# Attention followed by a long convolution on one core: shared-key scores and the last queries' value products in quarters of the TensorE array

## The chip, the cores and the metric

The kernel runs on one NeuronCore of a Trainium2 chip, in one launch. The metric is device time in microseconds (us). Engines go by their profile names: PE is TensorE's matmuls, PEld its loads of the stationary operand, DVE VectorE, ACT ScalarE, POOL GpSimd, SP SyncE, which issues most DMAs.

## The reference

Attention over 8 batches of 12 heads, 448 positions, head size 64, with one more term in the softmax's denominator, and on its output a gated convolution over the 448 positions by FFT:

```python
batch, n_heads, seq, head_dim = (8, 12, 448, 64)
scores = scale * np.matmul(q, k.transpose(0, 1, 3, 2))
m = np.max(scores, axis=-1, keepdims=True)
e = np.exp(scores - m)
attn = e / (np.sum(e, axis=-1, keepdims=True) + np.exp(-m) + 1e-09)
attn_out = np.matmul(attn, v)
x = attn_out.transpose(0, 2, 1, 3).reshape(B, S, H * D)          # 8 x 448 x 768
proj = x @ w_proj                                                # w_proj 768 x 2304
x1, x2, x3 = proj[..., :D], proj[..., D:2 * D], proj[..., 2 * D:]  # here D = 768
x2_conv = np.fft.irfft(np.fft.rfft(x2, n=S, axis=1) * np.fft.rfft(filter_fft, n=S, axis=0), n=S, axis=1)
return (x1 * x2_conv * x3) @ w_out                               # w_out 768 x 768
```

Inputs and output are float32; the kernel multiplies in bfloat16 and accumulates in float32.

## The kernel before

**Attention, pair by pair.** Two heads make a pair, numbered `i = 6 * b + hp` over 8 batches `b` and 6 pairs `hp`; head `u` of a pair is 0 or 1. In `kT` and `qT` the 64 features of head 0 lie on partitions 0 to 63 and those of head 1 on 64 to 127. The 448 keys of a head are three blocks of 128 (`t` = 1, 2, 3) and 64 left over. The left-over keys of both heads share block `t` = 0: its stationary operand is 128 x 128, with head 0's keys in one diagonal 64 x 64 block, head 1's in the other, and zeros elsewhere. `scores(0)` is thus one full-array matmul (L885), 128 rows by 128 columns, that streams 448 queries. `scores(t)` for the other blocks is two half-array matmuls (L883), one per head: 64 rows (features), 128 columns (keys), 448 queries; the heads lie on different row halves and write two banks of PSUM. `exps(t)` (ACT, L896 and L902) takes the exponential from PSUM into `e` (blocks 1 to 3, both heads) or `er` (block 0).

**Value products.** The exponentials are the stationary operand, 128 keys by 128 queries, and the values `vn` stream: 65 columns, 64 features and a column of ones for the denominator. `out_rests` (L914) does block 0: for four query blocks `n` and two heads one half-array matmul, 8 per pair. `out_rest(u)` (L922) does blocks 1 to 3 of head `u`: 12 full-array matmuls, 24 per pair. The fourth query block has 64 real queries; its other 64 columns are padding. The results of head 0 and 1 stand in two banks (`out_banks`). `norm` (DVE, L935 to L937) adds 1 to the denominators, takes reciprocals and multiplies into `xb`.

**The rest.** `x_dma` (SP, L989) turns three pairs of `xb` at once into `xT` by a DMA transpose; batch 0 does it on PE. `dense(b)` holds projections, spectra, inverse transforms and output projections (L1218, L1117, L1095, L1166, L1265, L1031), interleaved with the attention of later batches. After the last attention a flag on the smallest denominator is read and every engine takes a branch (L1573); the last output projections come after it.

**What sets the order.** Every step is a task, entered with `add(engine, cost, ...)`, what it needs, makes, and which buffers it takes and gives back. `Plan.run` plays the tasks on the engines with these costs, hands out the eight PSUM banks, and emits the instructions engine by engine. The table `plan.ORDER` holds each task's rank on its engine; the engines then run strictly in that order and wait on semaphores. A task's `rows` (64 or 128) tells the plan that a change between half and full array costs `SWITCH`. `fillers` puts idle matmuls (L1513) into PE gaps of the first 44 us of the plan.

Of the kernel before, what the change touches and what calls it, by code (L numbers as in the profile page):

```python
# [29 lines left out]
SX = 512  # L30
# [8 lines left out]
BLK_K = [FQ, FQ, SP, SP]  # L39


class Plan:
# [11 lines left out]
    LANDING = 1  # L54
    DELAY = (1.786, 2.77)
    EARLY = ((0.0, 0.0), (0.0, 0.0))
    TURN_ROOM = 1.6
# [8 lines left out]
    BRANCH = 0.0  # L66
    SWITCH = 0.093
# [16 lines left out]
    def add(self, eng, cost, want, emit, need=(), make=(), take=(), give=(), dma=0.0, run=256, n=1, after=0.0, begun=(), late=0.0, turn=False, part=None, keep=False, port=False, rows=128):  # L84
        want = self.ORDER[len(self.tasks)] if self.ORDER else want + self.SHIFT.get(part, 0.0)
        if eng == "SP":
            dma *= self.STRETCH
        if eng == "DVE" and port:
            cost += self.SHARED
        cost, dma, run, late = self.TIMES.get(len(self.tasks), (cost, dma, run, late))  # L90
        self.tasks.append((want, len(self.tasks), eng, cost, emit, need, make, take, give, dma, after, run, n, begun, late, turn, keep, port or eng == "POOL" and not dma, rows))

    def run(self):
# [21 lines left out]
        ahead = sum(t[2] == "ACT" and not t[16] for t in self.tasks)  # L115
        last = 0.0
# [80 lines left out]
        def ready(t):  # L197
            e = t[2]
            if not self.ORDER and t[10] > now + 1e-9:
                return False  # L200
            if t[16] and self.BRANCH:
                if ahead or "flag" not in when or max(last, when["flag"][0]) + self.BRANCH > now + 1e-9:
# [24 lines left out]
        while any(queue.values()):  # L227
            moved = False
            for e in queue:
# [30 lines left out]
                if e == "ACT" and not t[16]:  # L260
                    ahead, last = ahead - 1, now
                    heapq.heappush(events, now + self.BRANCH)
                if "flag" in t[6]:
                    heapq.heappush(events, end + self.BRANCH)
# [24 lines left out]
        full = self.fillers(order, gone)  # L289
        for i, (_, t) in enumerate(order):  # L290
            if i in full:
# [37 lines left out]
def kernel(  # L329
# [127 lines left out]
    flag = const.tile([1, 1], I32, name="flag")  # L457

    psum = psp.tile([128, 8 * 512], F32, name="psum")
# [33 lines left out]

# [1131 lines left out]
```

## Time and profile before

| | |
|---|---|
| runs | median 365.8 us, 365.61 to 366.53 |
| the profiled execution | 366.52 us, its span 364.7 us, granted TensorE clock 0.999 |
| PE, PEld | 356.0 us busy (98%), 211.6 (58%) |
| DVE, ACT, POOL | 259.6 us (71%), 263.8 (72%), 114.0 (31%) |
| DMA | 69.19 MB, mean 190 GB/s |
| shared-key scores (L885) | 48 matmuls of 128x448, 355 ns each |
| other scores (L883) | 288 of 64x448, 354 ns each |
| value products (L922, L914) | 1104 of 128x65, 194 ns, and 368 of 64x65, 191 ns, beside 64 that read the buffer in `wout_bf` |

The matmul's duration runs from its start to the end of its last result, while the next one is already under way; what it takes of PE's time is the distance between two starts. Times in a timeline count from the start of the span. A group `xN` of the timeline begins with its first instruction and ends with its last.

### The profile page before, as it was taken

To read this page: it belongs to the slowest core of one execution; us is meant where nothing else is said; L and a number is where in the kernel's file an instruction comes from. 1 tells how busy PE (TensorE), PEld (TensorE's weight loads), DVE (VectorE), ACT (ScalarE), POOL (GpSimd) and SP (SyncE) were. 2 spreads that over 40 slices of the span, in tenths; PEclk is the share of its full clock that TensorE was granted. 3 is DMA by queue.
4 is the path that set the end of the run, shared out by engine and by line. 5 is a ranking of instruction groups with operands and counts; after the bars stand their busy time and mean duration, and the time that the engine had idled before them with its cause. 6 is when DMAs were issued, how large, how long until landed. Compare 5 with 4: busy or idle time off the path is not lost. (4 is left out here: it accounts for less than half of the span.)

```text
span 364.7 us, 9337 instructions
## 1 busy us (share of the span) xinstructions
PE 356.0 (98%) x3599; PEld 211.6 (58%) x3600; DVE 259.6 (71%) x671; ACT 263.8 (72%) x453; POOL 114.0 (31%) x247
## 2 busy tenths in 40 slices
PE   8979999999999999999999999999999999999995
PEld 7656666656664555655565455655556556565552
DVE  6568489884889449797577568794578677858660
ACT  6879878677887588975779577878787875455443
POOL 6784463224724533444324533601020000000000
PEclk9999999999999999999999999999999999999999
DMA  8999999999999999999899999892983084143215
GB/s 219 262 245 234 257 229 205 227 199 172 220 265 257 228 250 247 227 279 212 225 240 244 271 235 221 231 216 66 190 155 68 2 151 111 43 88 88 86 49 174
DMA packets 135298, 69.19 MB, mean 190 GB/s; under 512 B 91917, under 2 KB 131664, under 8 KB 135248
## 3 DMA queue, kind: packets, MB, share of 16 engines
q1 hardware_dynamic: 130528, 62.90, 75.7%
q0 software_dynamic: 4480, 5.41, 8.7%
q8 instruction: 29, 0.48, 0.6%
q10 hardware_dynamic: 240, 0.23, 0.3%
q14 instruction: 21, 0.17, 0.2%
HBM read 43.86 MB, written 11.01 MB: 150 GB/s over the span
## 5 line engine op out<-in xcount | busy, mean ns | idle before, releaser
L896 ACT ACTIVATE e<-psum 128x896 bf16<-128x896 f32 x138 | 122.8, 924 | 20.6 <-PE psum L883 18.2
L1218 PE MATMUL psum<-xT,wproj_bf 128*128 128x448 bf16 x576 | 122.0, 353 | 0.0
L1218 PEld LDWEIGHTS <-wproj_bf 128*128 128x128 bf16 x576 | 54.4, 98 | 47.7 <-issue 3.5
L1031 PE MATMUL psum<-wout_bf,yT 128*128 128x384 bf16 (+2 forms) x287 | 54.2, 326 | 0.8 <-issue 0.6
L1117 PE MATMUL psum<-xf,wproj_bf 128*128 128x456 bf16 x216 | 45.4, 356 | 0.0
L922 PE MATMUL psum<-vn,e 128*128 128x65 bf16 x1104 | 45.2, 194 | 0.0
L922 PEld LDWEIGHTS <-e 128*128 128x128 bf16 x1104 | 39.5, 98 | 7.6 <-issue 3.4
L680 POOL CAST nat<-nat 112x512 bf16<-112x512 f32 x36 | 24.0, 671 | 62.1 <-DMA nat<-in_q_dram 61.9
L1344 ACT COPY osb<-psum 128x384 f32<-128x384 f32 (+2 forms) x56 | 25.8, 483 | 22.7 <-PE psum L1031 17.1
L883 PE MATMUL psum<-qT,kT 64*128 64x448 bf16 x288 | 41.6, 354 | 0.0
L1178 ACT CAST xs<-psum 113x384 bf16<-113x384 f32 (+1 forms) x64 | 29.6, 484 | 12.4 <-PE psum L1166 9.4
L1031 PEld LDWEIGHTS <-yT 128*128 128x128 bf16 x288 | 26.7, 98 | 20.1 <-issue 3.4
L1184 DVE TENSOR_TENSOR t<-xs,hrs 112x768 bf16<-112x768 bf16 (+1 forms) x64 | 35.3, 578 | 3.9 <-ACT xs L1178 3.7
L1234 DVE TENSOR_TENSOR g<-x,psum 128x448 bf16<-128x448 bf16 x42 | 25.8, 618 | 17.0 <-PE psum L1218 11.9
L937 DVE TENSOR_TENSOR xb<-psum,den 128x512 bf16<-128x512 f32 x48 | 33.2, 692 | 1.7
L1232 ACT CAST x<-psum 128x448 bf16<-128x448 f32 x42 | 22.3, 535 | 15.2 <-PE psum L1218 14.6
L712 POOL CAST vn<-nat 128x192 bf16<-128x192 f32 x58 | 23.1, 430 | 27.6 <-DMA nat<-in_v_dram 27.4
L1117 PEld LDWEIGHTS <-wproj_bf 128*128 128x128 bf16 x216 | 20.2, 98 | 18.8 <-issue 1.1
L1274 ACT CAST cr<-psum 128x452 bf16<-128x452 f32 x48 | 24.1, 544 | 8.1 <-PE psum L1265 7.2
L902 ACT ACTIVATE er<-psum 128x448 bf16<-128x448 f32 x46 | 25.4, 554 | 5.7 <-PE psum L885 5.4
L935 DVE TENSOR_SCALAR den<-psum 128x8 f32<-128x8 f32 x48 | 7.9, 164 | 24.1 <-PE psum L922 20.2
L700 POOL CAST nat<-nat 128x384 bf16<-128x384 f32 x29 | 16.6, 581 | 23.8 <-DMA nat<-in_k_dram 17.1
(138 smaller groups left out, 479.6 us busy)
## 6 DMA issues: line engine op xcount, KB each, us to landing
nat<-in_q_dram SPq DMA_DIRECT2D x47, 224.0 KB, 4.5
out_dram<-osb SPq DMA_DIRECT2D x23, 384.0 KB, 3.3
nat<-in_k_dram SPq DMA_DIRECT2D x41, 192.0 KB, 4.6
nat<-in_v_dram SPq DMA_DIRECT2D x41, 192.0 KB, 4.5
wproj_bf<-in_moe_w_proj_dram POOLq DMA_DIRECT2D x2, 1152.0 KB, 12.4
rests<-in_k_dram SPq DMA_DIRECT2D x8, 192.0 KB, 4.8
rests<-in_v_dram SPq DMA_DIRECT2D x8, 192.0 KB, 4.6
out_dram<-osb SPq DMA_DIRECT2D x8, 192.0 KB, 3.7
```

The costliest lines, as they stand in the source:

```text
L883: nc.tensor.matmul(sc[:, u, 0:S], kT[b % 2][c, hp, t, :], qT[b % 2][c, hp, :])
L896: nc.scalar.activation(to, of, AF.Exp, scale=SCALE)
L902: nc.scalar.activation(to, of, AF.Exp, scale=SCALE)
L922: nc.tensor.matmul(out_bank(u)[:, n, :], P["e"][1 + t][:, u * S + n * 128 : u * S + n * 128 + 128], vn[b % 2][:, hp, 4 * u + t, :], start= ...
L937: nc.vector.tensor_tensor(W["xb", b][:, hp].rearrange("p n (u d) -> p u n d", u=2), op[:, :, :, 0:DH], rec[:].unsqueeze(3).to_broadcast([1 ...
L1031: nc.tensor.matmul(ops[:n, : c.stop - c.start], y[:, dt, 0:n], wout_bf[:, dt, c], start=(dt == 0), stop=(dt == NDT - 1),)
L1117: nc.tensor.matmul(pps, wproj_bf[:, kt, D + dt * 128 : D + (dt + 1) * 128], W["xf", b][:, kt], start=(kt == 0), stop=(kt == NDT - 1),)
L1178: nc.scalar.copy(L["xs", par, ch][:K, pg % 2, :], L["Z", pg, ch][:K, :DCH])
L1184: nc.vector.tensor_tensor(t[:K], L["xs", par, ch][:K], h, op=ALU.mult)
L1218: nc.tensor.matmul(p[:, :S], wproj_bf[:, kt, 2 * part * D + dt * 128 : 2 * part * D + (dt + 1) * 128], xT()[:, kt, 0:S], start=(kt == 0), ...
L1234: nc.vector.tensor_tensor(g[:, dt, :], L["x1", dt], p[:, :S], op=ALU.mult)
L1344: (nc.vector.tensor_copy if half else nc.scalar.copy)(L["os", st][:n, c.start + lo : c.start + hi], L["O", st, ch][:n, lo:hi])
```

## The change

Four things change from batch 1 on (`QUADS`).

1. The shared-key scores of two neighbouring pairs are computed by one task, with four matmuls on quarters of the array (64 rows by 64 columns, 448 queries): per pair two, one per head, without the blocks of zeros. The second pair's heads are exchanged in their place among the columns, so that the four use the four quarters. Two PSUM banks are taken at once. `rest_values` exchanges the left-over values of the odd pairs accordingly, with three POOL copies for one.
2. The value products of the last 64 queries leave `out_rest`, which goes from 12 to 9 matmuls per head, and go into `out_rests`, in quarters: 64 keys by 64 queries. Head 0 goes to partitions 0 to 63, head 1 to 64 to 127; the two halves of the keys go to the two banks.
3. `norm` therefore first copies the second bank's part (65 columns) to SBUF and adds it to the first's. After `x_dma`, the new `x_shift` copies head 1's last 64 queries to their partitions.
4. A run of half-array tasks on PE that holds a quarter task is cut into quarters throughout (`narrow`, `parts`): a score matmul of 64 x 128 becomes two of 64 x 64.

The plan's costs, its model of the branch and its DMA delays get other values, and the whole table of ranks is new.

```diff
+QUADS = range(1, B)
-    LANDING = 1
-    DELAY = (1.786, 2.77)
+    LANDING = 1.84
+    DELAY = (0.897, 2.824)
-    SWITCH = 0.093
+    SWITCH = 0.105
...
         full = self.fillers(order, gone)
+        narrow, run = set(), []
+        for _, t in order:
+            if t[2] != "PE":
+                continue
+            if t[18] == 128:
+                run = []
+                continue
+            run.append(t[1])
+            if not self.quads.isdisjoint(run):
+                narrow.update(run)
...
-    plan.ORDER = (1, 0, 2, 125, 3, 4, 0, 0, 1, 2, 3, 4, 1, 9, 3, 0, ...
+    plan.ORDER = (1, 0, 1, 123, 3, 4, 0, 0, 3, 1, 2, 4, 2, 5, 16, 0, ...
-    plan.BRANCH = 3.5
+    plan.BRANCH = (2.5, 4.6, 2.0, 0.25)
...
+    def parts():
+        return [slice(0, 64), slice(64, 128)] if plan.narrow else [slice(0, 128)]
+
+    def rest_values(b):
+        if b not in QUADS:
+            nc.gpsimd.tensor_copy(vn[b % 2][:, :, 3, 0:DH], rests[:, 1])
+            return
+        lo, hi = slice(0, 64), slice(64, 128)
+        nc.gpsimd.tensor_copy(vn[b % 2][:, 0::2, 3, 0:DH], rests[:, 1, 0::2])
+        for to, of in ((lo, hi), (hi, lo)):
+            nc.gpsimd.tensor_copy(vn[b % 2][to, 1::2, 3, 0:DH], rests[of, 1, 1::2])
...
+        odd = hp % 2 if b in QUADS else 0
+        full = NST - 1 if b in QUADS else NST
         def scores(t):
             if t:
                 sc = pair(("sc", ("S", i, t)))
                 for u in range(2):
                     c = slice(64 * u, 64 * u + 64)
-                    nc.tensor.matmul(sc[:, u, 0:S], kT[b % 2][c, hp, t, :], qT[b % 2][c, hp, :])
+                    for m in parts():
+                        nc.tensor.matmul(sc[m, u, 0:S], kT[b % 2][c, hp, t, m], qT[b % 2][c, hp, :])
+            elif b in QUADS:
+                for g in range(2):
+                    for u in range(2):
+                        c, m = (slice(64 * x, 64 * x + 64) for x in (u, u ^ g))
+                        nc.tensor.matmul(
+                            bank(("hy", ("S", i + g, 0)))[m, 0:S], kT[b % 2][c, hp + g, 0, c], qT[b % 2][c, hp + g, :]
+                        )
...
         def out_rests():
-            for n in range(NST):
+            for n in range(full):
                 for u in range(2):
-                    c = slice(64 * u, 64 * u + 64)
+                    c = slice(64 * (u ^ odd), 64 * (u ^ odd) + 64)
+                    for m in parts():
+                        nc.tensor.matmul(
+                            out_bank(u)[m, n, :], P["e"][0][c, n * 128 + m.start : n * 128 + m.stop], vn[b % 2][c, hp, 3, :],
+                            start=(n == 0), stop=False,
+                        )
+            if full < NST:
+                q = slice(384, S)
+                half = [slice(0, 64), slice(64, 128)]
+                for u in range(2):
+                    c = half[u ^ odd]
                     nc.tensor.matmul(
-                        out_bank(u)[:, n, :], P["e"][0][c, n * 128 : n * 128 + 128], vn[b % 2][c, hp, 3, :],
-                        start=(n == 0), stop=False,
+                        out_bank(u)[half[u], full, :], P["e"][0][c, q], vn[b % 2][c, hp, 3, :], start=False, stop=False,
                     )
+                for t in (0, 2, 1):
+                    for r in range(2):
+                        for u in range(2):
+                            nc.tensor.matmul(
+                                out_bank(r ^ odd)[half[u], full, :],
+                                P["e"][1 + t][half[r], u * S + q.start : u * S + q.stop],
+                                vn[b % 2][half[r], hp, 4 * u + t, :],
+                                start=False, stop=False,
+                            )
 
         def out_rest(u):
-            for n in range(NST):
+            for n in range(full):
...
         def norm():
+            if full < NST:
+                nc.vector.tensor_copy(other, op[:, 1, full])
+                nc.vector.tensor_tensor(op[:, 0, full], op[:, 0, full], other, op=ALU.add)
...
+        def x_shift(gs):
+            nc.vector.tensor_copy(xT()[64:128, gs, 384:S], xT()[0:64, gs, S:SX])
```

Three places in the program's order show it. First, PE early in batch 2, where a shared-key score is issued (`kT`, `qT` keys and queries, `e` exponentials, `vn` values, `yT` the gated convolution that the output projection reads). Before, one full-array matmul stands between value products:

```order
L922 LDWEIGHTS e_100
L922 MATMUL psum<-vn_94,e_100 128x65
L885 LDWEIGHTS kT_89
L885 MATMUL psum<-qT_91,kT_89 128x448
L922 LDWEIGHTS e_99
L922 MATMUL psum<-vn_94,e_99 128x65
```

Now the run of half-array tasks there begins with a score block cut into quarters, and the quarter group follows it (each load and matmul that is shown of L925 and L930 stands four times):

```order
L989 LDWEIGHTS e_100
L989 MATMUL psum<-vn_94,e_100 128x65
L925 LDWEIGHTS kT_89
L925 MATMUL psum<-qT_91,kT_89 64x448
...
L930 LDWEIGHTS kT_89
L930 MATMUL psum<-qT_91,kT_89 64x448
...
L1115 LDWEIGHTS yT
L1115 MATMUL psum<-wout_bf,yT 128x384
```

The shared scores went from a full-array run into a half-array run, and two pairs' scores stand at one place. Second, PE at the value products of a pair of batch 1 (`er` the exponentials of block 0, `e` those of blocks 1 to 3). Before, eight L914 matmuls are followed, here after a score block, by the 24 of L922:

```order
L914 LDWEIGHTS er_103
L914 MATMUL psum<-vn_94,er_103 128x65
L883 LDWEIGHTS kT_90
L883 MATMUL psum<-qT_92,kT_90 128x448
...
L922 LDWEIGHTS e_99
L922 MATMUL psum<-vn_94,e_99 128x65
L922 LDWEIGHTS e_101
L922 MATMUL psum<-vn_94,e_101 128x65
```

Now twelve quarters of L964 (of which one is shown) are followed by two of L973 and by four for each key block of L979, and the full-array products of L989 come after:

```order
L964 LDWEIGHTS er_102
L964 MATMUL psum<-vn_94,er_102 64x65
...
L973 LDWEIGHTS er_102
L973 MATMUL psum<-vn_94,er_102 64x65
...
L979 LDWEIGHTS e_96
L979 MATMUL psum<-vn_94,e_96 64x65
...
L979 LDWEIGHTS e_98
L979 MATMUL psum<-vn_94,e_98 64x65
...
L989 LDWEIGHTS e_96
L989 MATMUL psum<-vn_94,e_96 128x65
```

Work of all four key blocks went into the quarter run, and of the full-array products nine instead of twelve per head are left. Third, DVE at a normalisation of batch 1. Before:

```order
L604 COPY qT_92<-psum 128x448
L593 COPY kT_90<-psum 128x512
L935 TENSOR_SCALAR den_108<-psum 128x8
L936 RECIPROCAL den_108<-den_108 128x8
L937 TENSOR_TENSOR xb<-psum,den_108 128x2x4x64
```

Now:

```order
L642 COPY qT_92<-psum 128x448
L1002 COPY other<-psum 128x65
L1003 TENSOR_TENSOR psum<-psum,other 128x65
L1005 TENSOR_SCALAR den_108<-psum 128x8
L1006 RECIPROCAL den_108<-den_108 128x8
L1007 TENSOR_TENSOR xb<-psum,den_108 128x2x4x64
```

Two instructions came in ahead of each normalisation.

More of the change, by code (lines that the diff above doesn't have):

```diff
@@ L65 @@
     PORT = 0.16
-    BRANCH = 0.0
-    SWITCH = 0.093
+    BRANCH = ()
+    SWITCH = 0.105
     NBANKS = 8
@@ L82, in __init__, with add @@
         self.rows = {}
-    def add(self, eng, cost, want, emit, need=(), make=(), take=(), give=(), dma=0.0, run=256, n=1, after=0.0, begun=(), late=0.0, turn=False, part=None, keep=False, port=False, rows=128):
+        self.quads = set()
+        self.narrow = False
+    def add(self, eng, cost, want, emit, need=(), make=(), take=(), give=(), dma=0.0, run=256, n=1, after=0.0, begun=(), late=0.0, turn=False, part=None, keep=False, port=False, rows=128, quad=False):
+        if quad:
+            self.quads.add(len(self.tasks))
         want = self.ORDER[len(self.tasks)] if self.ORDER else want + self.SHIFT.get(part, 0.0)
@@ L114, in run @@
         clock = 0.0
-        ahead = sum(t[2] == "ACT" and not t[16] for t in self.tasks)
-        last = 0.0
+        ahead = {e: sum(t[2] == e and not t[16] for t in self.tasks) for e in ("ACT", "PE")}
+        last = {"ACT": 0.0, "PE": 0.0}
         landed = {"SP": [], "POOL": []}
@@ L201, in ready @@
             if t[16] and self.BRANCH:
-                if ahead or "flag" not in when or max(last, when["flag"][0]) + self.BRANCH > now + 1e-9:
+                if "flag" not in when:
+                    return False
+                at = when["flag"][0] + self.BRANCH[0]
+                if e != "PE":
+                    if ahead["ACT"] or ahead["PE"]:
+                        return False
+                    at = max(when["flag"][0] + self.BRANCH[1], last["ACT"] + self.BRANCH[2], last["PE"] + self.BRANCH[3])
+                if at > now + 1e-9:
                     return False
@@ L259, in run @@
                 heapq.heappush(events, end)
-                if e == "ACT" and not t[16]:
-                    ahead, last = ahead - 1, now
-                    heapq.heappush(events, now + self.BRANCH)
+                if e in ahead and not t[16]:
+                    ahead[e] -= 1
+                    last[e] = now if e == "ACT" else end
+                    for x in self.BRANCH:
+                        heapq.heappush(events, last[e] + x)
                 if "flag" in t[6]:
-                    heapq.heappush(events, end + self.BRANCH)
+                    for x in self.BRANCH:
+                        heapq.heappush(events, end + x)
                 for k in t[13]:
@@ L457 @@
     flag = const.tile([1, 1], I32, name="flag")
+    other = const.tile([128, DH + 1], F32, name="other")
     psum = psp.tile([128, 8 * 512], F32, name="psum")
@@ L926, in out_rest @@
                         start=False,
-                        stop=(n == NST - 1 and t == 1),
+                        stop=(n == full - 1 and t == 1),
                     )
@@ L952, in rests @@
         def rests(j, w):
-            add("PE", 0.125, w, T[j]["rests"], need=[("e", j), ("ones", j // NHP % 2), "pads", ("v", j), ("vr", j // NHP)], make=[("ER", j)],
-                take=[("op", j)], give=[("er3" if j in THIRD else "er", (j, 0))], rows=64)
+            add("PE", 0.235 if j // NHP in QUADS else 0.125, w, T[j]["rests"], need=[("e", j), ("ones", j // NHP % 2), "pads", ("v", j), ("vr", j // NHP)], make=[("ER", j)],
+                take=[("op", j)], give=[("er3" if j in THIRD else "er", (j, 0))], rows=64, quad=j // NHP in QUADS)
         for t in range(4):
             w = tau(i, t / 4 if i or t else 1.0)
-            add("PE", 0.195 if t else 0.19, w, lambda t=t: scores(t),
-                need=[("kT", i), ("qT", i)] + ([("S", i - 1, 2)] if b and not t else []) + ([] if i or t else ["kT0"])
-                + ([("S", i, t - 1) if t > 1 else ("S", i - 1, 3)] if t and (i or t > 1) else []),
-                make=[("S", i, t)], take=[(ring(t), ("S", i, t))], rows=64 if t else 128)
+            if t or b not in QUADS:
+                add("PE", 0.195 if t else 0.19, w, lambda t=t: scores(t),
+                    need=[("kT", i), ("qT", i)] + ([("S", i - 1, 2)] if b and not t else []) + ([] if i or t else ["kT0"])
+                    + ([("S", i, t - 1) if t > 1 else ("S", i - 1, 3)] if t and (i or t > 1) else []),
+                    make=[("S", i, t)], take=[(ring(t), ("S", i, t))], rows=64 if t else 128)
+            elif not odd:
+                add("PE", 0.22, w, lambda t=t: scores(t),
+                    need=[(x, j) for j in (i, i + 1) for x in ("kT", "qT")] + [("S", i - 1, 2)],
+                    make=[("S", j, 0) for j in (i, i + 1)], take=[("hy", ("S", j, 0)) for j in (i, i + 1)], rows=64, quad=True)
             if t == host:
@@ L1015, in attention @@
                 add("SP", 1.53, w, x_dma, need=[("xb", NHP * b + h) for h in ps] + old,
-                    make=[m for h in ps for m in (("X", NHP * b + h), ("xT", b, h))], dma=(0.0, 0.5, 0.9, 1.33)[len(ps)], run=0.2, late=0.05, turn=True)
+                    make=[m for h in ps for m in (("X", NHP * b + h), (x_of(h), b, h))], dma=(0.0, 0.5, 0.9, 1.33)[len(ps)], run=0.2, late=0.05, turn=True)
+                if b in QUADS:
+                    add("DVE", 0.22, w + 5.0, lambda ps=ps: x_shift(slice(ps.start, ps.stop)), need=[("x0", b, h) for h in ps],
+                        make=[("xT", b, h) for h in ps])
         else:
```

18 lines of the change are left out of this document (10 added, 8 removed).

## The prediction

> **What bounds the kernel now.** I read the page first, then a long window in the middle, then who waits for whom on TensorE, then short stretches of TensorE's timeline. The page gives the shares:
>
> ```profile
> span 364.7 us, 9337 instructions
> PE 356.0 (98%) x3599; PEld 211.6 (58%) x3600; DVE 259.6 (71%) x671; ACT 263.8 (72%) x453; POOL 114.0 (31%) x247
> PEclk9999999999999999999999999999999999999999
> ```
>
> TensorE (PE) is busy for 98% of the span at the full granted clock; VectorE (DVE) and ScalarE (ACT) have more than a quarter of the span free. The window from 40 to 350 us and the list of TensorE's waits say where the remaining 2% lies:
>
> ```profile
> 40.00:350.00 310.00, 310.00 (x3061) 181.10 (x3060) 227.05 (x582) 226.96 (x396) 88.84 (x183) 1.00 0.84 186
> ```
>
> ```profile
> PE psum L576 <- POOL ldm L535: 2.0, 2, 1.9
> PE psum L1521 <- DVE zero L1500: 1.1, 1, 1.1
> PE psum L1031 <- issue: 0.6, 1, 0.6
> ```
>
> For 310 us TensorE has no gap at all, and its waits (the three longest are shown) belong to the first 30 us, where casts of loads are late, and to the last projections after the branch. "Busy" alone doesn't prove a bound, because matmuls overlap in the records. The starts prove it:
>
> ```profile
> 239.79 1.31 PE L1218 MATMUL psum<-xT,wproj_bf 128*128 128x448 bf16 x6
> 240.94 0.35 PE L885 MATMUL psum<-qT,kT 128*128 128x448 bf16 x1
> 241.12 1.46 PE L1031 MATMUL psum<-wout_bf,yT 128*128 128x384 bf16 x8
> 242.52 0.55 PE L883 MATMUL psum<-qT,kT 64*128 64x448 bf16 x4
> 242.91 0.28 PE L914 MATMUL psum<-vn,er 64*128 64x65 bf16 x8
> 243.13 0.90 PE L922 MATMUL psum<-vn,e 128*128 128x65 bf16 x24
> 243.87 0.81 PE L1031 MATMUL psum<-wout_bf,yT 128*128 128x384 bf16 x4
> 244.51 0.35 PE L1218 MATMUL psum<-xT,wproj_bf 128*128 128x448 bf16 x1
> ```
>
> The first column is the start, the second the time from first start to last end. From start to start a full-array matmul of 448 columns takes 1.15/6 = 0.19 us, one of 384 takes 0.64/4 = 0.16, one of 65 takes 0.74/24 = 0.031. One of 448 columns lasts 0.35 us by itself, so the next is always begun before the last one ends. TensorE is paced by the columns it streams. What shortens that stream between 40 and 350 us shortens the kernel one for one, as long as nobody makes TensorE wait.
>
> The same rows price the other two things that the change touches. On half arrays (64 rows), two matmuls run side by side: four of 448 columns have starts that span 0.55 - 0.354 = 0.196 us (0.354 is the mean duration of one, below), so a pair takes 0.196; eight of 65 columns span 0.28 - 0.191 = 0.09 for three steps, 0.030 per pair, 0.12 in all. And a change between full and half array costs: eight of 384 columns should take 8 x 0.16 = 1.28 but the half-array run starts 1.40 us after them, 0.1 us a switch.
>
> ```profile
> L922 PE MATMUL psum<-vn,e 128*128 128x65 bf16 x1104 | 45.2, 194 | 0.0
> L883 PE MATMUL psum<-qT,kT 64*128 64x448 bf16 x288 | 41.6, 354 | 0.0
> L885 PE MATMUL psum<-qT,kT 128*128 128x448 bf16 x48 | 16.9, 355 | 0.1
> L914 PE MATMUL psum<-vn,er 64*128 64x65 bf16 x368 | 13.3, 191 | 0.4 <-DVE xb L937 0.4
> ```
>
> **The change part by part**, for the 42 pairs of batches 1 to 7.
>
> 1. *Shared-key scores.* 42 full matmuls of 448 columns go: 42 x 0.19 = 8.0. In their place come 21 groups of four quarter-array matmuls. If a group takes what a half-array pair takes, 21 x 0.196 = 4.1. Gain **3.9 us**. The other bound is two pairs in turn, 21 x 0.39 = 8.2, no gain. The pair row is the nearest (same columns, same two banks written); I take it.
>
> 2. *Value products of the last 64 queries.* Per pair 24 full matmuls become 18: 252 fewer x 0.031 = **7.8 us** gained.
>
> 3. *They come back in quarters.* Per pair 8 half-array matmuls (0.12 us) become 26 quarter-array ones, in seven groups of at most four. If a group takes 0.031 like a pair, 0.217; if its four run as two pairs, 0.43. I take 0.034, near the lower end, as a group must issue four loads and four matmuls where a pair issues two: 0.238 - 0.12 = 0.118, x 42 = **5.0 us** lost (bounds 4.1 and 13.2).
>
> 4. *Switches.* In the program's order TensorE changes between full and half (or quarter) array 160 times before and 174 times now: 14 x 0.1 = **1.4 us** lost.
>
> 5. *Entry into quarters.* 56 half-array runs hold a quarter group and are therefore cut into quarters throughout. Their first stationary load has nothing to hide behind, since the array has just been switched, and narrower loads are slower here:
>
> ```profile
> L922 PEld LDWEIGHTS <-e 128*128 128x128 bf16 x1104 | 39.5, 98 | 7.6 <-issue 3.4
> L1166 PEld LDWEIGHTS <-ft 113*113 113x113 bf16 x24 | 3.0, 132 | 1.6 <-issue 0.4
> ```
>
> A load of 113 columns takes 34 ns longer than one of 128. Scaled to 64 columns that is 19 ns, x 56 = **1.0 us** lost (0 to 1.9).
>
> 6. *The other scores in those runs.* 97 of the 144 half-array score pairs become four quarters of 64 columns of keys each. At the pair's price nothing changes; at 5 ns for two more loads and matmuls, **0.5 us** lost.
>
> 7. *Start.* The order now holds 90 idle filler matmuls instead of 72; they stand where the order expects TensorE to have nothing. Ten of them span 0.72 us, 0.055 from start to start, so up to 18 x 0.055 = 1.0 us more emptiness in the first 44 us. Batch 0 is computed as before and loads are ordered anew; either sign is possible, I take **0.5 us** lost (bounds -1 and +1).
>
> ```profile
> 10.69 0.72 PE L1513 MATMUL psum<-idle 128*128 128x128 bf16 x10
> ```
>
> 8. *VectorE.* Each of 42 normalisations gets a copy and an addition of 65 columns from PSUM, and 14 copies move the second head's last queries to the upper partitions after the DMA transpose.
>
> ```profile
> 150.93 0.17 DVE L935 TENSOR_SCALAR den<-psum 128x8 f32<-128x8 f32 x1 [0.85 <-PE psum L922]
> 151.13 0.20 DVE L936 RECIPROCAL den<-den 128x8 f32<-128x8 f32 x1
> 151.36 0.69 DVE L937 TENSOR_TENSOR xb<-psum,den 128x512 bf16<-128x512 f32 x1
> ```
>
> From 8 to 512 columns the time goes from 0.17 to 0.69, so 65 columns take about 0.23: 84 x 0.23 + 14 x 0.2 (the reciprocal's row) = 22 us. Between 40 and 350 us VectorE goes from 227 to some 249 of 310 us, 80%. It mostly waits for TensorE today:
>
> ```profile
> DVE den L935 <- PE psum L922: 20.2, 24, 2.1
> DVE g L1234 <- PE psum L1218: 12.3, 16, 2.1
> ```
>
> That slack is the cover, and I price this at nothing. The output banks come free 0.46 us later in each pair, out of 5.9 us from pair to pair (48 shared scores in 285 us):
>
> ```profile
> L885 PE MATMUL psum<-qT,kT x48: 349/353/364, 9.9 to 294.9; 128*128 128x448 bf16 x48
> ```
>
>  Without that cover, every tenth of a microsecond that a normalisation holds TensorE up costs 42 x 0.1 = 4.2 us.
>
> 9. *The moved copy waits for a DMA.* The 14 copies stand in VectorE's queue behind a transpose that takes 3.2 to 5.8 us to land. In half of the places the next row is the fold of the same batch, which needed that landing anyway; in the others products of the spectrum or a normalisation stand behind it.
>
> ```profile
> DMA to landing us min/median/max: 3.2/3.7/5.8
> ```
>
> GpSimd gets 14 more small casts in a 31% busy engine: nothing. The tail after the branch keeps its matmuls, only the widths of the last two groups swap: nothing.
>
> Sum: -3.9 - 7.8 + 5.0 + 1.4 + 1.0 + 0.5 + 0.5 = **-3.3 us**. The profiled execution took 366.5 us (364.7 of span and 1.8 around it) and would take 363.2; the median of the runs is 365.8, 0.7 lower, so I predict **362.5 us**.
>
> [...]
>
> **The rivals.**
>
> *A. The four quarters of the shared scores don't run together* (about 366.6 us). They are the only groups in which both row halves write into one bank, on different partitions; all others keep one bank to a row half. If such a group takes 0.39, part 1 gains nothing: -3.3 + 4.1 = +0.8, within 0.3% of before. No row of before has two row halves in a bank, so nothing here speaks for or against it. [...]
>
> *B. The small groups are paced by their loads* (about 371 us, slower). Place: the 26 small matmuls of each pair. If a group takes 0.062, as two pairs in turn or as a load that isn't hidden, part 3 costs 42 x (0.434 - 0.12) = 13.2 instead of 5.0: -3.3 + 8.2 = +4.9, 370.7. It decides against the change from a group time of about 0.045 us on (each 10 ns are 2.9 us). Against it: four matmuls of 113 columns with 113-column loads
>
> ```profile
> 6.92 0.38 PE L802 MATMUL psum<-ident_bf,sb 113*113 113x113 bf16 x4
> ```
>
> span 0.38 - 0.218 (one of them) = 0.16 for three steps, 0.054 each, so 113 columns load in no more than that, and 64 in about 0.031, just the time of 65 streamed columns. For it: there is no room left, and a group has four such loads.
>
> *C. Column halves don't overlap at all.* Then the 97 cut score pairs double as well: +4.9 + 4.1 + 97 x 0.196 = +28, 394 us. Nothing in the trace excludes it; two row halves do overlap, and I give it little.
>
> *D. VectorE becomes late.* If the later normalisations or the copies behind the transposes hold up TensorE by 0.08 us a pair, that is 3.4 us and the gain is gone: 366. Against it: no TensorE wait for VectorE after 40 us in the list.
>
> **How the numbers follow.** About 0.3%, 1.1 us, is what a measurement of this kernel can tell from no change. The forecast (gain of 1.1 to 7 us) gets 0.70; A 0.09; B 0.10; C 0.03; D 0.08. Faster is the forecast, 0.70; within is A and most of D, 0.16; slower is B, C and the rest of D, 0.14. The forecast's own lower end is parts 3, 5, 6, 7 at their lower bounds: -3.9 - 7.8 + 4.1 + 1.4 - 1 = -7.2, 358.6. Upwards the range has to take in A and D: to 367.5. B and C, 0.13, and a little of the forecast stay outside.
>
> **What would show it.** The four shared-score matmuls start within a few ns of each other and the next run 0.2 us later (A: 0.39). The 26 small matmuls of a pair take 0.22 to 0.26 us from first start to the end of the run (B: over 0.4). Runs cut into quarters cost some 20 ns more at their entry. TensorE still has no wait between 40 and 350 us (D: waits for VectorE appear). The value products number 900 instead of 1152, and VectorE's busy time goes to about 281 us. Wrong would make it: a group time over 0.045 us, or a start that waits some microseconds longer for loads.

## The result, and the profile after

The changed kernel takes 375.1 us (median of 4 runs, 374.79 to 375.62), the kernel before beside it 365.9. The ratio is 1.025, 95% interval 1.0237 to 1.0268: 9.2 us slower, where 3.3 us less was forecast. Three runs of two kernels further down (roomy_orders_2, later_orders) were over 1.5% longer than the fastest run of their kernel; medians and intervals leave them out.

The page of the changed kernel, its lines on the span, the engines, TensorE's clock and the DMA engines:

```profile
span 373.8 us, 11003 instructions
PE 355.4 (95%) x4358; PEld 211.4 (57%) x4358; DVE 277.8 (74%) x769; ACT 261.9 (70%) x452; POOL 115.4 (31%) x261
PE   8889999499999999999899999999999999999995
PEclk9999999879999999999999999999999999999999
DMA  8999999989999999999999999979982056134035
```

TensorE is busy for 95% of a longer span, has a hole in the eighth slice, and its clock drops there (0.8 and 0.7 in the eighth and ninth slices). The long window that had no gap before now has gaps of 9.5 us in all. The list of TensorE's waits begins with the two largest causes; the third line stands at 27 us, ahead of the window:

```profile
40.00:350.00 310.00, 300.51 (x3734) 174.55 (x3733) 241.69 (x665) 221.05 (x384) 90.76 (x197) 0.99 0.87 184
```

```profile
PE psum L925 <- DMA kT<-nat: 5.5, 1, 5.5
PE psum L1250 <- DMA x<-xb: 2.3, 2, 1.7
PE psum L873 <- DVE xb L1007: 1.2, 1, 1.2
```

The two largest entries wait for DMA transposes: keys of batch 2 once (`kT`, turned from `nat`, the rows as they were loaded), and the turned spectra twice (`x`, near 145 and 181 us). TensorE's timeline at the first (start, time from first start to last end), and the window behind it:

```profile
66.20 1.30 PE L1302 MATMUL psum<-xT,wproj_bf 128*128 128x448 bf16 x6
67.43 0.38 PE L925 MATMUL psum<-qT,kT 64*64 64x448 bf16 x4
73.35 0.59 PE L925 MATMUL psum<-qT,kT 64*64 64x448 bf16 x4 [5.54 <-DMA kT<-nat]
...
75.62 2.43 PE L1302 MATMUL psum<-xT,wproj_bf 128*128 128x448 bf16 x6
```

```profile
73.00:79.00 6.00, 5.65 (x89) 3.37 (x90) 1.52 (x5) 1.98 (x3) 1.97 (x6) 0.50 0.35 81
```

Six projections of 448 columns take 1.30 us ahead of the wait and 2.43 behind it: the granted clock (third number from the end of the window's row) is 0.50 for these 6 us. One place thus costs 5.5 us of waiting and about 3 us of slow matmuls.

The quarters themselves do what the forecast said. Here is one run of them in the timeline, and the groups that replace those shown of before:

```profile
93.64 1.46 PE L1179 MATMUL psum<-wproj_bf,xf 128*113 128x384 bf16 x8
95.04 0.29 PE L964 MATMUL psum<-vn,er 64*64 64x65 bf16 x12
...
95.26 0.38 PE L925 MATMUL psum<-qT,kT 64*64 64x448 bf16 x3
95.45 0.39 PE L930 MATMUL psum<-qT,kT 64*64 64x448 bf16 x4
95.77 0.72 PE L989 MATMUL psum<-vn,e 128*128 128x65 bf16 x18
```

```profile
L989 PE MATMUL psum<-vn,e 128*128 128x65 bf16 x852 | 36.0, 195 | 0.0
L930 PE MATMUL psum<-qT,kT 64*64 64x448 bf16 x84 | 7.7, 353 | 0.0
```

From 95.04 to 95.26 go the 26 small matmuls of a pair (0.22 us), from 95.26 to 95.45 a score block in four quarters, from 95.45 to 95.77 the shared scores of two pairs (0.19 us, L930) and the switch back to the full array.

To compare kernels, I divide TensorE's time from its first to its last matmul's start. Where a distance between two starts exceeds what its columns take at full pace (448 in 0.189 us) by over 154 ns (94 for a switch, 60 to spare), all that exceeds counts as *waiting*; the rest is the *stream*. At half clock a matmul of 448 columns passes that limit (0.37 us from start to start in the six projections above), and one of 384 does by estimate, at twice its 0.16 us; so some of the slow clock counts as waiting. Other fair ways to draw the limit move a sum by up to about 1 us. All is in us, the time a median, the rest of one profiled run each:

| kernel | time | stream | waits to 40 | 40 to 350 | after 350 |
|---|---|---|---|---|---|
| before | 365.9 | 353.5 | 4.9 | 0.0 | 1.3 |
| after | 375.1 | 350.1 | 3.9 | 13.2 | 0.8 |
| old_work_new_order | 378.0 | 359.7 | 4.5 | 5.9 | 1.1 |
| loads_order | 365.4 | 349.3 | 2.7 | 3.8 | 1.0 |
| all_orders | 371.4 | 347.9 | 5.4 | 7.7 | 0.7 |
| loads_early | 371.5 | 349.9 | 3.3 | 8.7 | 1.1 |
| loads_late | 372.2 | 350.1 | 4.0 | 9.7 | 1.1 |
| short_norm | 374.6 | 350.2 | 5.1 | 11.3 | 0.8 |
| longer_norm | 368.4 | 353.8 | 3.7 | 3.0 | 1.1 |
| values_alone | 373.5 | 351.8 | 7.5 | 6.1 | 0.7 |
| half_after | 366.4 | 350.3 | 5.0 | 2.0 | 1.0 |
| half_before | 370.0 | 355.1 | 6.0 | 1.0 | 1.2 |

Before to after: stream -3.4, waits +11.7, behind the last matmul +0.7 (3.6 to 4.3 us). Of the changed kernel's slow clock, about 2.8 us in all, some 1.7 us stand in the 13.2 of waits and 1.1 in the stream of 350.1.

### The profile page after: what moved, and what is told of

The parts are those of the page before. It is cut to its first block, busy times and chain, and to the rows that moved or that the text cites. A ratio compares the mean times of both kernels' runs of the same rounds, so it can differ in the third digit from the quotient of the medians.

```text
span 373.8 us, 11003 instructions
## 1 busy us (share of the span) xinstructions
PE 355.4 (95%) x4358; PEld 211.4 (57%) x4358; DVE 277.8 (74%) x769; ACT 261.9 (70%) x452; POOL 115.4 (31%) x261
## 5 line engine op out<-in xcount | busy, mean ns | idle before, releaser
L925 PE MATMUL psum<-qT,kT 64*64 64x448 bf16 (+1 forms) x482 | 48.1, 364 | 6.6 <-DMA kT<-nat 5.5
L1268 DVE TENSOR_TENSOR t<-xs,hrs 113x768 bf16<-113x768 bf16 (+1 forms) x64 | 36.7, 592 | 3.6 <-ACT xs L1262 3.5
L718 POOL CAST nat<-nat 112x512 bf16<-112x512 f32 x36 | 22.9, 641 | 50.2 <-DMA nat<-in_q_dram 49.9
L1262 ACT CAST xs<-psum 113x384 bf16<-113x384 f32 (+1 forms) x64 | 29.0, 489 | 13.4 <-PE psum L1250 11.3
L989 PE MATMUL psum<-vn,e 128*128 128x65 bf16 x852 | 36.0, 195 | 0.0
L989 PEld LDWEIGHTS <-e 128*128 128x128 bf16 x852 | 30.5, 98 | 7.4 <-issue 4.9
L1316 ACT CAST x<-psum 128x448 bf16<-128x448 f32 x42 | 22.7, 539 | 11.8 <-PE psum L1302 10.7
L925 PEld LDWEIGHTS <-kT 64*64 64x64 bf16 (+1 forms) x482 | 14.8, 103 | 27.1 <-issue 16.4
L951 ACT ACTIVATE er<-psum 128x448 bf16<-128x448 f32 x46 | 24.2, 551 | 4.8 <-PE psum L930 3.6
L1274 DVE TENSOR_TENSOR yh<-t 112x384 bf16<-112x384 bf16 (+1 forms) x64 | 23.9, 391 | 0.6 <-DVE cv L1378 0.2
## 6 DMA issues: line engine op xcount, KB each, us to landing
wproj_bf<-in_moe_w_proj_dram POOLq DMA_DIRECT2D x2, 1152.0 KB, 13.2
```

Source lines behind the costliest of these rows:

```text
L925: nc.tensor.matmul(sc[m, u, 0:S], kT[b % 2][c, hp, t, m], qT[b % 2][c, hp, :])
L989: nc.tensor.matmul(out_bank(u)[:, n, :], P["e"][1 + t][:, u * S + n * 128 : u * S + n * 128 + 128], vn[b % 2][:, hp, 4 * u + t, :], start= ...
L1262: nc.scalar.copy(L["xs", par, ch][:K, pg % 2, :], L["Z", pg, ch][:K, :DCH])
L1268: nc.vector.tensor_tensor(t[:K], L["xs", par, ch][:K], h, op=ALU.mult)
```

## The experiments

**First: the quarters, or the order?** My theory after the traces is that the quarters save what was forecast, but the new order needs transfers sooner than they come. The rival is that the quarters bring the waits (two pairs' keys at once, longer normalisations, copies behind transposes). Three kernels separate them.

*old_work_new_order.*

```diff
-    plan.ORDER = (1, 0, 2, 125, 3, 4, 0, 0, 1, 2, ...
+    plan.ORDER = (1, 0, 1, 123, 3, 4, 0, 0, 3, 1, ...
...
-  ([("S", i - 1, 2)] if b and not t else [])
+  ([("S", i - 1, 2)] if b and not t and hp % 2 == 0 else [])
```

> The kernel before, with its own matmuls, tile widths and copies, but every engine runs its tasks in the order of the changed kernel (the shared-key scores of both pairs of a quarter task stand side by side at that task's place, as two full-array matmuls; the copies behind the transposes do not exist). Theory (the new order has no room for late transfers): TensorE, which had no wait between 40 and 350 us, waits there for a key transpose near 67 us and for turned spectra near 145 and 181 us, 8 to 14 us in all, and the time is 370 to 379 us, since the stream is about 3.4 us longer than with quarters. Rival (the quarters themselves make the waits: two pairs' keys needed at once, longer normalisations, copies behind transposes): few waits after 40 us, 365 to 369 us.

Measured: 377.96 us, ratio 1.030 (1.0254 to 1.0353). The wait for keys came back, near 70 us, without a single quarter:

```profile
PE psum L883 <- DMA kT<-nat: 3.5, 1, 3.5
PE psum L835 <- DVE xb L937: 1.6, 1, 1.6
```

The waits for turned spectra did not, so the waits come to 5.9 us and not 8 to 14. The stream rose by 6.2 us, more than I expected. In this order the full-array scores stand inside half-array runs (192 switches against 160, 3 us), the plan puts 104 idle fillers where it put 72 before (1.8 us at 0.055 each), and the half clock around the end of the wait (0.50 for 3.4 us) leaves about 1 us in the stream. The order without the quarters costs 12 us, and it made the wait for the keys. That the order alone makes the waits for the spectra is not shown: this stream is 9.6 us longer than the changed kernel's.

*loads_order.* Of 2128 ranks 372 differ, all of them SyncE's and GpSimd's. Some of them, changed kernel to this one: cast of pair 12's queries 52 to 50 and load of `w_out` 55 to 51 on GpSimd; transpose of pair 12's keys 49 to 47 and load of pair 15's values 47 to 61 on SyncE.

```diff
-    plan.ORDER = (1, 0, 1, 123, 3, 4, 0, 0, 3, 1, ...
+    plan.ORDER = (1, 2, 0, 92, 3, 4, 0, 0, 3, 1, ...
```

> The changed kernel with TensorE, VectorE and ScalarE in exactly its own order; only the order of SyncE's loads, transposes and stores and of GpSimd's casts and loads is searched anew, with transfers assumed to land 1.3 us later than the changed kernel's plan assumes. Theory (order without room for late transfers): the wait of 5.5 us near 67 us and the clock dip behind it go, the waits between 40 and 350 us fall from 13 us to under 4, 363 to 368 us. Rival (the quarters themselves): the waits stay where they are, 373 to 377 us.

Measured: 365.35 us (363.7 to 368.31, ten runs), ratio 0.998 (0.9952 to 1.0014). That is 9.7 us below the changed kernel with TensorE's, VectorE's and ScalarE's orders untouched; only idle fillers differ, by three. The chain to the keys follows for both, first SyncE and GpSimd of the changed kernel (start, time of the issue or cast):

```profile
45.45 0.48 SPq L698 DMA_DIRECT2D rests<-in_k_dram  x1
...
60.44 1.67 SPq L682 DMA_TRANSPOSE qT<-nat  x1
...
63.33 5.86 SPq L689 DMA_TRANSPOSE kT<-nat  x2
```

```profile
44.51 0.82 POOL L899 DMA_DIRECT2D wproj_bf<-in_moe_w_proj_dram  x1
...
57.98 1.29 POOL L702 CAST nat<-rests 64x384 bf16<-64x384 f32 x2 [2.86 <-DMA rests<-in_k_dram]
...
61.39 0.82 POOL L904 DMA_DIRECT2D wout_bf<-in_moe_w_out_dram  x1
```

then SyncE and GpSimd of loads_order:

```profile
43.58 0.47 SPq L698 DMA_DIRECT2D rests<-in_k_dram  x1
...
55.46 1.32 SPq L682 DMA_TRANSPOSE qT<-nat  x1
58.35 1.22 SPq L689 DMA_TRANSPOSE kT<-nat  x1
```

```profile
44.18 0.82 POOL L899 DMA_DIRECT2D wproj_bf<-in_moe_w_proj_dram  x1
...
55.38 0.82 POOL L904 DMA_DIRECT2D wout_bf<-in_moe_w_out_dram  x1
56.25 0.50 POOL L702 CAST nat<-rests 64x384 bf16<-64x384 f32 x1
```

In the changed kernel the left-over keys of batch 2 (`rests`) are asked for 0.9 us behind a megabyte of `w_proj`, and land 12.4 us later, 0.5 us behind it; the cast waits, the transposes follow, and the keys' transpose is issued 1.9 us behind `w_out` and lands at 73.31, 10 us later. In loads_order `rests` goes 0.6 us ahead of `w_proj` and lands in 4.8 us; the keys' transpose is issued 5 us sooner and lands at 66.51. The kernel before had the same order of the two loads, with `rests` 1.5 us ahead, and its transpose landed at 67.04. SyncE's lines and GpSimd's line of before:

```profile
43.34 0.37 SPq L660 DMA_DIRECT2D rests<-in_k_dram  x1
...
60.06 1.27 SPq L651 DMA_TRANSPOSE kT<-nat  x1
```

```profile
44.87 0.82 POOL L861 DMA_DIRECT2D wproj_bf<-in_moe_w_proj_dram  x1
```

*all_orders.*

```diff
-    plan.ORDER = (1, 0, 1, 123, 3, 4, 0, 0, 3, 1, ...
+    plan.ORDER = (4, 0, 2, 114, 0, 2, 1, 0, 1, 2, ...
```

> The changed kernel with the orders of all five engines searched anew under later landings; all computation is that of the changed kernel. Theory: the stream stays 3 to 4 us shorter than before the change and waits between 40 and 350 us are under 2 us, 359 to 364 us, faster than before the change. Rival (the quarters themselves make the waits): 370 us or more.

Measured: 371.43 us, ratio 1.0145 (1.0074 to 1.0216). The theory's 359 to 364 us were missed. The stream is short, 347.9, but four new waits of 1.2 to 1.6 us begin at 26, 69, 118 and 163 us, for a cast, for VectorE and for keys. This kernel decides nothing between the theories, since its waits are other ones than the changed kernel's.

**Second: which places, and is VectorE in it?**

*loads_early and loads_late* take loads_order's ranks for one side of 90 us of the plan and the changed kernel's for the other. The lines show the changed kernel's ranks, then those of loads_early (132 differ) and of loads_late (240).

```diff
-    plan.ORDER = (1, 0, 1, 123, 3, 4, 0, 0, 3, 1, ...
+    plan.ORDER = (1, 2, 0, 123, 3, 4, 0, 0, 3, 1, ...
+    plan.ORDER = (1, 0, 1, 92, 3, 4, 0, 0, 3, 1, ...
```

> The changed kernel, with the order of loads_order on SyncE and GpSimd only for the tasks that the changed kernel's plan starts before 90 us; all later ones, and the other engines throughout, keep the changed kernel's order. Theory (two separate places without room): the wait of 5.5 us near 67 us and the slow clock behind it go, the waits for turned spectra near 145 and 181 us stay, 365 to 369 us. Rival (what follows after 90 us is late because the start is, or the wait only moves): no wait after 40 us left, or 372 us and more.

> The counterpart: SyncE and GpSimd keep the changed kernel's order for the tasks that its plan starts before 90 us, and take that of loads_order for the later ones. Theory: the wait near 67 us and the slow clock behind it stay, the waits near 145 and 181 us go, 371 to 374 us. Rival (later waits follow from the early one): they stay too, 375 us.

Measured: 371.51 us (ratio 1.0157, 1.0111 to 1.0202) and 372.16 (1.0167, 1.0121 to 1.0213). TensorE's longest waits of loads_early and of loads_late:

```profile
PE psum L1250 <- DMA x<-xb: 3.2, 2, 2.3
PE psum L925 <- DMA kT<-nat: 2.6, 1, 2.6
```

```profile
PE psum L925 <- DMA kT<-nat: 4.4, 2, 4.0
PE psum L925 <- DMA qT<-nat: 1.1, 1, 1.1
```

As expected, each half keeps the waits of the side that it left alone, so there are two separate places; loads_late has a new wait of 1.1 us for queries at 193 us. Not as expected, loads_early also waits 2.6 us for the keys, with loads_order's own issue order up to there, and its time lies above the expected 365 to 369 us. Its transpose was issued at 59.08 and landed at 69.56, as `w_out` took 13.1 us instead of 10.7. So even the better order is on the edge, and in this run a slower transfer went with the wait's return; the ten runs of loads_order spread over 4.6 us.

*longer_norm* lengthens the normalisations of the kernel before, *short_norm* shortens those of the changed one by leaving out the copy and the addition of the second bank's part, and *values_alone* is a part of the change in the old order.

```diff
+            if b:
+                for u in range(2):
+                    nc.vector.tensor_copy(other, op[:, u, NST - 1])
             rec = dens[b % 2][:, hp]
```

> The kernel before, order and all, with one thing added: each of the 42 normalisations of batches 1 to 7 begins with two more VectorE copies of 65 columns from PSUM into a buffer that nobody reads, so it gets as long as the changed kernel's. The prediction's part 8 (VectorE's slack covers it): VectorE's busy time rises by some 19 us, TensorE still has no wait between 40 and 350 us, 365 to 367 us. Rival (the output banks and what stands behind on VectorE have no such room): TensorE waits behind normalisations, a tenth of a microsecond a pair or more, 370 us or more.

```diff
-            if full < NST:
-                nc.vector.tensor_copy(other, op[:, 1, full])
-                nc.vector.tensor_tensor(op[:, 0, full], op[:, 0, full], other, op=ALU.add)
```

> The changed kernel in its own order without the copy and the addition of 65 columns at the start of each of the 42 normalisations (left out: the second bank's half of the last 64 queries' value products). If the longer normalisations take part in the changed kernel's waits: VectorE gets 19 us of work less, the waits on TensorE between 40 and 350 us fall from 13 to 7 to 11 us, 369 to 373 us. If they come from the order of the loads alone: the waits stay at 67, 145 and 181 us, 374 to 375 us. If VectorE is the whole cause: waits under 3 us, 363 us.

```diff
+PAIRED = ()
...
-            elif b in QUADS:
+            elif b in PAIRED:
...
-            if t or b not in QUADS:
+            if t or b not in PAIRED:
```

> Of the change only the value products of the last 64 queries in quarters, the cut of the runs that hold them, the longer normalisation and the copies behind the transposes; shared-key scores as full-array matmuls pair by pair. Every engine keeps the order of the kernel before, and each new copy stands ahead of the first product that reads it. By the prediction's parts 2, 3, 5 and 6 the stream is some 1.5 to 3 us shorter, and if VectorE's slack covers parts 8 and 9 the time is 363 to 365 us. Rival (an order made for shorter normalisations has no room for longer ones): TensorE's waits between 40 and 350 us come to 3 us or more, 366 to 373 us.

Measured: longer_norm 368.38 us, ratio 1.0067 (1.0046 to 1.0088); short_norm 374.57, ratio 1.023 (1.0205 to 1.026), not to be told from the changed kernel; values_alone 373.53, ratio 1.0215 (1.015 to 1.028). In the changed kernel's order VectorE's added work is not what TensorE waits for. In the old order it is not free: 2.3 us, between my two expectations, through waits of half a microsecond:

```profile
PE psum L884 <- DVE xb L941: 1.2, 2, 0.6
PE psum L1170 <- DMA x<-xb: 0.6, 1, 0.6
```

values_alone has the stream that was expected (351.8, 1.7 us less), but its time is the rival's: it pays 6.1 us of waits between 40 and 350 us, most of them short and for VectorE, and 2.6 more at the start. Of these, 0.9 us are a wait for `w_proj` at 37 us, 0.4 a longer wait for a cast at 19 us, and about 0.4 slow clock behind that; the rest I did not place. The old order has no room either for tasks that got longer.

**Third: is it the transfers?** The prediction did not use the page's DMA row of the kernel before. It follows, with the windows from 35 to 140 us of before, after and loads_order (the last two numbers are the DMA share of 16 engines and GB/s):

```profile
DMA  8999999999999999999899999892983084143215
```

```profile
35.00:140.00 105.00, 105.00 (x1098) 64.12 (x1097) 78.65 (x203) 81.03 (x137) 44.55 (x93) 1.00 1.09 227
```

```profile
35.00:140.00 105.00, 98.78 (x1284) 59.76 (x1281) 79.95 (x220) 75.27 (x128) 41.37 (x92) 0.97 1.03 211
```

```profile
35.00:140.00 105.00, 103.43 (x1382) 62.96 (x1381) 84.74 (x232) 80.18 (x137) 46.41 (x104) 1.00 1.12 231
```

The DMA engines are full in all three (shares of 1.09, 1.03 and 1.12); the kernel before kept them at 227 GB/s and TensorE without a wait. *half_loads* and *half_after* keep the changed kernel's order and leave out many of the rows that are loaded between 35 and 140 us and later: 64 partitions are loaded where 112 or 128 were.

```diff
-   nc.sync.dma_start(src.rearrange("p (u c) -> p u c", u=2), rows(x, b, hp))
+   nc.sync.dma_start(src[0:h].rearrange("p (u c) -> p u c", u=2), rows(x, b, hp, h))
...
-   nc.gpsimd.dma_start(wout_bf, moe_w_out.rearrange("(t p) c -> p t c", p=128))
+   nc.gpsimd.dma_start(wout_bf[0:64], moe_w_out.rearrange("(t p) c -> p t c", p=128)[0:64])
```

> The changed kernel in its own order, with less to transfer: from batch 2 on, the loads of queries, keys and values bring 64 partitions instead of 112 or 128 (all but the first few, whose buffers must be filled once), and the last third of w_proj and w_out are loaded for 64 partitions. Left out: the other rows, which keep older values or zeros; every engine does the same instructions on them. Theory (the first 140 us are bound by the transfers, and the new order needs them sooner than they come): the waits between 40 and 350 us fall from 13 us to under 3, the clock stays up, 361 to 365 us. Rival (the waits come from the order of instructions, casts and issues, whatever the transfers take): waits of 8 us or more, 370 us or more.

Measured: 367.74 us, ratio 1.0052 (1.0025 to 1.0078), with 4.7 us of waits between 40 and 350 us; both lie between the theory's ranges and the rival's. But the zeros for the rows left out stood first on VectorE and held TensorE's first matmul back from 1.1 to 6.0 us, a lead for the loads. So it was made again with the zeros written later (half_after), and also for the kernel before (half_before):

> The changed kernel in its own order with the cut in transfers of half_loads, but without its late start: from batch 2 on, loads of queries, keys and values bring 64 partitions instead of 112 or 128 (all but the first few), the last third of w_proj and w_out are loaded for 64 partitions; the zeros for the others are written by VectorE while it waits for the filter and by GpSimd behind its load of w_out. Left out: the other rows of these inputs. Theory (transfers come later than the new order needs them): waits between 40 and 350 us under 4 us, 361 to 365 us. Rival (half_loads gained by its late start, which gave the loads 5 us of lead): the wait near 67 us is back at 3 us or more, 368 us or more.

> The same cut in transfers in the kernel before, in its own order. Left out: the same rows. Theory: the kernel before has no wait between 40 and 350 us that could go, and its time falls by no more than what its start waits for loads, 363 to 366 us; half_after is then 1 to 4 us below it, which is what the sum of the prediction says of TensorE's stream. Rival (the quarters bring waits of their own, not by transfers): half_after is not below half_before.

Measured: half_after 366.36 us (ratio to before 1.0032, 1.0011 to 1.0054), half_before 369.98 (1.0116, 1.0087 to 1.0144). The window of half_after and two of its waits:

```profile
35.00:140.00 105.00, 104.50 (x1407) 64.38 (x1405) 83.45 (x235) 80.52 (x138) 49.31 (x103) 1.00 0.85 179
```

```profile
PE psum L875 <- DVE xb L1011: 1.9, 1, 1.9
PE psum L1254 <- DMA x<-xb: 0.4, 1, 0.4
```

With the same order, fewer bytes take the waits between 40 and 350 us from 13.2 to 2.0 us and the wait for the keys away. The time falls by 8.7 us, not quite into the expected 361 to 365 us, since a wait at 27 us got longer (first row; 1.2 us in the changed kernel) and up to 1.7 us go to slow clock behind it. half_before missed its expected 363 to 366 us: the kernel before had no such waits to lose, and now waits for VectorE near 28 us (1.2 and 0.7 us), with a granted clock of 0.50 for 3.4 us behind it; that the added zeros made these waits is likely and not shown. Side by side, half_after is 3.6 us faster than half_before. This agrees with the forecast's sum, but both kernels are disturbed at their start, so it is support for the sum and not a measurement of it.

**Fourth: is there an order without these waits?** Four more searches keep all computation of the changed kernel: roomy_orders and roomy_orders_2 from two starts, later_orders from loads_order on, third_search with slower early transfers.

```diff
-    plan.ORDER = (1, 0, 1, 123, 3, 4, 0, 0, 3, 1, ...
+    plan.ORDER = (2, 0, 1, 125, 1, 3, 0, 0, 1, 2, ...
+    plan.ORDER = (0, 1, 0, 93, 2, 3, 1, 0, 1, 2, ...
+    plan.ORDER = (1, 2, 0, 129, 3, 4, 0, 0, 3, 1, ...
+    plan.ORDER = (2, 1, 0, 150, 1, 3, 0, 0, 2, 1, ...
```

> The changed kernel, all its computation, with the orders of all engines searched anew: normalisations at the 1.72 us that the trace shows (the changed kernel's plan has 1.49), transfers that land up to 1.6 us later each by a random amount, four draws at once. Theory (the order's room decides): stream 348 to 350 us, waits between 40 and 350 us under 2 us, 359 to 363 us, faster than before the change. Rival (no order has room for the quarters' extra VectorE work and two pairs' keys at once): waits of 4 us or more as in loads_order and all_orders, 365 us or more.

> The same search from another start, to see how far the result hangs on one order. Theory: 359 to 364 us, waits between 40 and 350 us under 3 us. Rival as for roomy_orders: 365 us or more.

> The changed kernel; up to 88 us of the plan every engine keeps the order of loads_order, after that all five orders are searched anew with transfers landing up to 1.6 us later at random and normalisations at 1.72 us. Theory: what loads_order still waits after 90 us (some 1.5 us) goes, 361.5 to 364.5 us, faster than before the change. Rival (new orders bring new waits, as in all_orders and roomy_orders): 365 us or more.

> The changed kernel with all five orders searched anew, now with every transfer of the first 75 us and all of GpSimd's loads taking 4 to 8% longer than the changed kernel's plan has them, beside random late landings, and normalisations at 1.72 us. Theory: if the plan's transfers of the first 75 us were what the earlier searches had wrong, waits between 40 and 350 us under 3 us and 359 to 364 us. Rival (TensorE's stream is ahead of the transfers whatever the order): waits of 5 us or more between 40 and 140 us, 366 us or more.

Measured, in this order: 372.44 us (1.0132 to 1.0192), 372.21 (1.0124 to 1.0197), 368.61 (1.0052 to 1.0117), 374.16 (1.0213 to 1.027); the intervals are of the ratio to before. All four missed what their theories expected. They have waits between 40 and 350 us of 9.5, 10.3, 4.5 and 8.7 us, in the first two mostly from 40 to 120 us. One row of roomy_orders:

```profile
PE psum L925 <- DVE g L1318: 3.3, 1, 3.3
```

Such waits were not where the searches' model had them, so its picture of what comes when is not good enough to search by at this level of room; which part of it is wrong stays open. No kernel with the quarters is faster than the kernel before; loads_order equals it. That no order has room for the quarters is thus not excluded.

## Why the prediction was wrong

- *Parts 1, 2: right.* A group of four shared-score quarters takes 0.190 us (0.196 was forecast), so -4.0; 900 full-array value products remain, so -7.8.
- *Part 3: right, smaller.* 26 quarters take 0.213 us where the eight took 0.128: 0.085 x 42 = 3.6 lost, not 5.0.
- *Parts 4 to 6: right.* There are 14 more switches at 0.094, 1.3 us; a run cut into quarters costs 13 ns at its entry (0.213 for its first score block, 0.200 before), 0.7 in all; further cut blocks cost nothing (two take 0.402, against 0.389 before, and the entry alone explains the 13 ns).
- These items come to -6.2, and 18 fillers of part 7 to +1.0; with the 1.1 us of slow clock that the stream holds, that is -4.1, against a stream 3.4 us shorter. That 3.4 lies so near the forecast's 3.3 is partly luck, since the slow clock is in it. Without slow clock, loads_order's stream is 4.2 us shorter than before's; between half_before and half_after, which both have some, lie 4.8.
- *Part 7: the start.* Waits before 40 us fell by 1.0. But behind the last matmul 0.7 us were added, where the tail was priced at nothing. The runs say where they come from: the last matmuls now stream 512 columns and those of before 256, and old_work_new_order, without a quarter, has both the 512 columns and the 4.3 us. It came with the order.
- *Part 8: mis-sized, and its cover not proved.* A normalisation went from 1.13 to 1.72 us (42 of each, from the first instruction's start to the last one's end), 0.59 and not 0.46 more; VectorE's busy time came to 277.8 (281 forecast). longer_norm prices it at 2.3 us in the old order; in the new one short_norm shows nothing of it.
- *Part 9.* VectorE waited 4.1 us for transposes in three places; no wait of TensorE hangs on it in the list.
- **The step that failed** is the premise ahead of all parts, "as long as nobody makes TensorE wait", with its expectation that TensorE "still has no wait between 40 and 350 us". I looked for who might wait on VectorE and priced the new order by its fillers and its 14 copies. I did not follow the loads on SyncE's and GpSimd's queues, where old_work_new_order, loads_order and half_after place the cost: 13.2 us of waits between 40 and 350 us, 1.7 of them matmuls at half clock, and 1.1 us more of half clock in the stream. "Wrong would make it ... a start that waits some microseconds longer for loads" named the cause, but at the start, where the waits fell.
- *Rivals A, B and C are refuted*: a group of four shared-score quarters takes 0.190 us, a group of small quarters about 0.030, and column halves overlap (two cut score blocks take 0.402 us). In A's case, L930 has two row halves writing one bank, on different partitions, and its group takes no longer than the 0.196 us of a half-array pair. D had the sign right, by luck: it named VectorE, and without the longer normalisations (short_norm) the time stays.

## What to carry to other kernels

A busy share of 98% on one engine says nothing of the room on the others: read the DMA row too (here a share of 1.09 and 227 GB/s from 35 to 140 us), and where it is full, a shorter stream may only meet its data sooner (here 3.4 us less of stream, and waits of 13.2 us between 40 and 350 us). A change that comes with a new order is two changes; run the old work in the new order and the new work with only the loads moved before judging either. In an order tuned to no waits, room is part of what was tuned, and a few microseconds of room lost at one landing can outweigh every matmul saved: the keys that landed at 73.31 us and not at 67.04 cost 5.5 us of waiting and about 3 us of slow matmuls, against 3.4 us of stream.

## What the runs showed of the hardware

- **Around the end of waits of 1.9 to 5.5 us, TensorE's granted clock was 0.50 for 3.4 or 6.8 us.** In the changed kernel it was 0.50 from 72.5 to 79.4 us, beginning 0.8 us before the wait of 5.5 us ended; in loads_early for 3.4 us (69.3 to 72.7), beginning 0.3 us before one of 2.6 us ended; in half_after for 3.4 us, beginning 0.8 us after one of 1.9 us ended. The wait's length alone does not decide: 3.3 us in roomy_orders went with 6.8 us of half clock, 3.5 us in old_work_new_order with 3.4, and a wait of 1.9 us at 18 us in the kernel before had no such sequel (its clock was 1.00 from 18 to 28 us). What does decide was not shown. The window of loads_early:

```profile
69.50:72.50 3.00, 2.90 (x54) 2.30 (x55) 0.80 (x4) 1.04 (x2) 1.64 (x4) 0.50 1.20 290
```

- **The same small load took 12.4 us behind a large one and 4.8 us ahead of it.** The 192 KB of left-over keys, issued 0.9 us behind a megabyte on another queue that took 12.8 us, landed 0.5 us behind it; in loads_order they were issued 0.6 us ahead. Elsewhere they took 13.2 us in old_work_new_order and 11.9 in loads_late behind it, and 5.8 in the kernel before ahead of it.
